# Summing the first batch's keys with products on both partition halves, a new order of the first tokens' attention, a third bank for expert 1, and two later pieces in other slots

## The chip, the cores and the metric

The kernel runs on one core of a Trainium2 chip. The metric is the device time of one execution in microseconds. A profile gives the span from the first to the last instruction, which is 1.5 to 2 us shorter than the timed figure; spans are compared with spans and times with times. A run counts as slow when it is over 1.5% above the fastest of the same kernel.

Engines are called PE (matrix products), DVE (VectorE), ACT (ScalarE) and POOL (GpSimd).

## The reference, cut to what matters

```python
# q, k, v: 8 batches, 8 heads, 576 tokens, 64 per head; four experts, 512 -> 1024 -> 512
k_p = k.reshape(B, H, Sp, 8, D).mean(axis=3)          # keys and values: means of 8 neighbours, 72 left
v_p = v.reshape(B, H, Sp, 8, D).mean(axis=3)
attn = softmax(q @ k_p^T / sqrt(D))
x = (attn @ v_p), heads side by side                  # 4608 tokens x 512
for e in range(4):
    out += p[:, e:e + 1] * (relu(x @ w1[e]) @ w2[e])  # "up" and "down" products
```

## The kernel before

The attention of the first 512 tokens (four rows of 128) runs before anything else. Nothing else is there for PE to do, because the first up products need its result. From then on the kernel walks chunks of tokens and experts. In each step PE does up and down products, and pieces of the next batch's attention are put into numbered slots between them. Most products are done by a scheme with seven block products in place of eight, for which DVE first adds or subtracts blocks of weights and of activations ("combine").

The first batch's keys lie on 64 partitions, nine neighbouring tokens in each. A 0/1 matrix (`takes`) sums groups of eight by nine accumulating products. The values already lie on both partition halves, and their products alternate between the halves:

```python
def sum_pool(raw, hs):                      # keys: one half of the partitions
    for h in range(hs.start, hs.stop, 2):
        s_ps = work_bank()
        for r in range(ROWS):               # ROWS = 9
            nc.tensor.matmul(s_ps[0:SP, 0:n], lhsT=takes[0:PR, r], rhs=raw[:, h:h + 2, r, :], ...)

def sum_values(g):                          # values: two halves, two banks, in turn
    banks = [work_bank()[0:SP, 0:n] for _ in range(2)]
    for r in range(ROWS):
        for half in range(2):
            ps = slice(half * PR, (half + 1) * PR)
            nc.tensor.matmul(banks[half], lhsT=takes[ps, r], rhs=raws[("vraw", 0)][ps, g, :, r, :], ...)

def idle(n):                                # dummy products; nothing reads their results
    w_ps = work_bank()
    for _ in range(n):
        nc.tensor.matmul(w_ps, lhsT=zeros[:, 0:P], rhs=zeros)
```

The order of the first attention, from the key sums on. `scores_first(group, tok)` does scores and exponential of four heads and 256 tokens; `context` and `context_half` do a row's products with the values and then a division on DVE; `turn` transposes a row for the up products:

```python
sum_keys(lo); keys(0, lo); sum_keys(hi); scores_first(0, 0); keys(0, hi)
sum_values(0); scores_first(1, 0); context_half(0, 0); sum_values(1)
scores_first(0, 1); turn_half(0, 0); context_half(0, 1); idle(3); turn_half(0, 1)
context(0, 1); scores_first(1, 1); up_first(range(0, 4), first)
turn(0, 1); context(0, 2); idle(1); up_first(range(0, 4), second); context(0, 3)
... # rest of up_first, turn(0, 2), turn(0, 3)
up(0, 0, range(FCH), half)                  # the second half: 256 tokens, 8 blocks
```

Two more places matter: the banks of the up products, and the slots of later pieces.

```python
banks = units[1] if n == NT else units[1] + chains[1:]      # 2 banks for 512 wide, 3 for 256 wide
...
turn_of("up", 2)                            # first_chunk: which of the two banks comes first
...
usual = dict(queries=-8, keys=-9, values=-2, ...)
plans[BUSY + 1] = dict(usual, values=4, v=(5, 8, 12, 16))   # fourth batch: its key fold in slot -9
... ((12, 15, 22, 19), weight_sums(2)) ...                  # the fourth combine of expert 2 in slot 19
```

The softmax here doesn't subtract the row's maximum and nothing guards it: scores larger than these inputs give would overflow.

## Time and profile before

| | before |
|---|---|
| time, median of the first 3 runs | 497.9 us (497.85 to 498.71) |
| span of the profile | 495.8 us |
| PE busy | 488.6 us, 99% |
| PE idle | 7.2 us |

The prediction below shows the lines on which it rests: the busy times, the chain, PE's timeline of the first 22 us and the one late wait. One view that it does not show is DVE's timeline where the first attention ends (start, length, engine and line, what, then the idle time before it and what ended it):

```profile
17.92 0.20 DVE L397 RECIPROCAL inv<-att_first 128x8 f32<-128x8 f32 x1
18.15 0.69 DVE L398 TENSOR_TENSOR x_tok<-att_first,inv 128x512 bf16<-128x512 f32 x1
19.47 0.21 DVE L397 RECIPROCAL inv<-att 128x8 f32<-128x8 f32 x1 [0.63 <-PE att L435]
19.71 0.69 DVE L398 TENSOR_TENSOR x_tok<-att,inv 128x512 bf16<-128x512 f32 x1
```

The reader sees the last two divisions (reciprocal and product, 0.9 us together). The third row's is over before the last row's can start: DVE waits 0.63 us for the last context.

### The profile page before, as it was taken

Reading aid. Unit: us, or ns where it says so; the run is one execution under the profiler, and the core shown is the slowest. Engines: PE = TensorE matmul, PEld = TensorE weight load, DVE = VectorE, ACT = ScalarE, POOL = GpSimd, SP = SyncE. Lnnn points to the kernel's source line nnn. Section 1 sums busy time; section 2 is a strip of 40 time slices with the busy share of each in tenths; the row PEclk is TensorE's granted clock in tenths of the full one; section 3 lists DMA queues with packets and bytes.
Section 4 is the critical chain, followed back from the end, with each engine's and each line's share of the span. In section 5 each row is a group of like instructions: output and inputs, shape, how many; then the busy total and the mean of one; then the engine's idle time right before and its main releaser. Section 6 shows DMA issues by size and latency. Waiting matters only on the chain.

```text
span 495.8 us, 11453 instructions
## 1 busy us (share of the span) xinstructions
PE 488.6 (99%) x4663; PEld 407.1 (82%) x4663; DVE 377.1 (76%) x756; ACT 302.7 (61%) x561; POOL 114.4 (23%) x112
## 2 busy tenths in 40 slices
PE   8999999999999999999999999999999999999996
PEld 5856468888888888888888888888888888888885
DVE  5567889799768975788669876896679766976674
ACT  4666536865685568656775667567665566556650
POOL 8230413232352154114421262111000100011010
PEclk9999999999999999999999999999999999999999
DMA  9999996998679659553974398130211010004003
GB/s 199 210 207 203 205 164 92 119 73 97 76 112 62 95 61 146 47 78 37 156 73 67 47 138 80 36 65 22 76 23 22 22 65 1 13 22 86 1 1 85
DMA packets 101779, 41.95 MB, mean 85 GB/s; under 512 B 73808, under 2 KB 100176, under 8 KB 101728
## 3 DMA queue, kind: packets, MB, share of 16 engines
q0 software_dynamic: 56896, 22.42, 40.4%
q1 hardware_dynamic: 43728, 17.77, 17.6%
q10 hardware_dynamic: 1104, 1.05, 0.6%
q8 instruction: 36, 0.59, 0.5%
q14 instruction: 15, 0.12, 0.1%
HBM read 45.69 MB, written 9.44 MB: 111 GB/s over the span
## 4 chain that ended last, share of the span: by engine, by line
PE 95%; DVE 2%; ACT 1%; issue 1%; ACTq 0%
PE o_ps L724 40%; PE unit L656 39%; PE unit L583 5%; PE o_ps L750 3%; PE att L382 2%; PE unit L332 1%; PE unit L782 1%; PE att L435 1%; DVE acc L799 1%; PE unit L598 0%; PE unit L306 0%; DVE H L637 0%; DVE kp L285 0%; PE att L489 0%; PE att L472 0%
## 5 line engine op out<-in xcount | busy, mean ns | idle before, releaser
L799 DVE SCALAR_TENSOR_TENSOR acc<-o_ps,p_all,acc 128x256 f32<-128x256 f32 (+1 forms) x285 | 127.1, 486 | 54.3 <-PE o_ps L724 36.1
L724 PEld LDWEIGHTS <-H 128*128 128x128 bf16 x1320 | 129.1, 98 | 16.2 <-issue 0.3
L656 PEld LDWEIGHTS <-w_bf 128*128 128x128 bf16 x1024 | 97.8, 98 | 15.9 <-issue 4.5
L637 DVE CUSTOM_DVE_ANT_0 H<-unit,partial 128x512 bf16<-128x512 f32 x128 | 87.4, 685 | 25.5 <-PE unit L656 20.9
L724 PE MATMUL o_ps<-w_bf,H 128*128 128x256 bf16 x792 | 102.6, 273 | 0.0
L656 PE MATMUL unit<-xT,w_bf 128*128 128x256 bf16 x672 | 96.4, 273 | 0.8 <-ACT unit L669 0.8
L671 ACT COPY partial<-unit 128x512 f32<-128x512 f32 x128 | 72.0, 589 | 33.2 <-PE unit L656 32.9
L738 POOL TENSOR_TENSOR acc<-acc,addend 128x512 f32<-128x512 f32 x24 | 30.4, 1265 | 258.3 <-ACT addend L736 201.3
L656 PEld LDWEIGHTS <-wu_bf 128*128 128x128 bf16 x768 | 73.3, 98 | 10.0 <-issue 1.5
L656 PE MATMUL unit<-xs,wu_bf 128*128 128x256 bf16 x512 | 76.9, 273 | 0.0
L724 PE MATMUL o_ps<-wt_bf,H 128*128 128x256 bf16 x528 | 68.4, 273 | 0.0
L724 PEld LDWEIGHTS <-S 128*128 128x128 bf16 x528 | 51.7, 98 | 6.4
L677 ACT ACTIVATE H<-unit 128x512 bf16<-128x512 f32 x64 | 38.2, 597 | 29.6 <-PE unit L656 29.3
L673 ACT ACTIVATE H<-unit 128x512 bf16<-128x512 f32 x64 | 38.8, 607 | 27.0 <-PE unit L656 27.0
L669 ACT COPY unit<-unit 128x512 f32<-128x512 f32 x64 | 37.4, 584 | 17.2 <-PE unit L656 14.7
L656 PE MATMUL unit<-xs,w_bf 128*128 128x256 bf16 x256 | 38.5, 273 | 0.0
L797 ACT ACTIVATE acc<-o_ps,p_all 128x256 f32<-128x256 f32 x72 | 30.2, 471 | 12.1 <-PE o_ps L724 10.8
L151 POOL DMA_DIRECT2D vraw<-in_v_dram x20 | 29.3, 1466 | 24.1 <-DMA vraw<-in_v_dram 23.8
L151 POOL DMA_DIRECT2D kraw<-in_k_dram x20 | 25.9, 1295 | 37.4 <-DMA kraw<-in_k_dram 37.4
L724 PE MATMUL o_ps<-wt_bf,S 128*128 128x256 bf16 x264 | 34.2, 273 | 0.0
L724 PE MATMUL o_ps<-w_bf,S 128*128 128x256 bf16 x264 | 34.2, 273 | 0.0
L656 PE MATMUL unit<-xT,wu_bf 128*128 128x256 bf16 x224 | 33.6, 272 | 0.0
(148 smaller groups left out, 516.7 us busy)
## 6 DMA issues: line engine op xcount, KB each, us to landing
out_dram<-acc SPq DMA_DIRECT2D x32, 256.0 KB, 4.2
w_bf<-in_moe_w_dram POOLq DMA_DIRECT2D x7, 1024.0 KB, 23.5
q_sb<-in_q_dram POOLq DMA_DIRECT2D x7, 512.0 KB, 9.8
vraw<-in_v_dram POOLq DMA_DIRECT2D x22, 144.0 KB, 6.5
kraw<-in_k_dram POOLq DMA_DIRECT2D x21, 144.0 KB, 5.3
w_bf<-in_moe_w_dram POOLq DMA_DIRECT2D x2, 512.0 KB, 8.8
wt_bf<-in_k_dram POOLq DMA_DIRECT2D x2, 288.0 KB, 6.8
wt_bf<-in_v_dram POOLq DMA_DIRECT2D x4, 144.0 KB, 5.6
```

The lines of the kernel that those rows point to most:

```text
L151: nc.gpsimd.dma_start(out=raw[:], in_=rows_of(src, b, 2 * part, 2 * part + 2), accum_op=ALU.add if part else ALU.bypass)
L583: nc.tensor.matmul(out_ps, lhsT=w1_bf[:, e, kc, fc * P:(fc + 1) * P], rhs=xT[:, kc, at], start=(kc == 0), stop=(kc == KC - 1), skip_group_ ...
L637: nc.vector._custom_dve(TENSOR_ADD_SAT, out=dst, in0=ps, in1=part, s0=LARGEST, s1=0.0)
L656: nc.tensor.matmul(ps[:, n * HN:(n + 1) * HN], lhsT=lhs[:, kc, f:f + P], rhs=rhs[:, kc, :], start=(not grows and n == 0 and kc == 0), stop ...
L669: nc.scalar.copy(out=units[unit][1][:], in_=ps)
L671: nc.scalar.copy(out=part[:, step - 2], in_=ps)
L673: nc.scalar.activation(out=quarter(0, 0), in_=ps, func=ACT.Relu)
L677: nc.scalar.activation(out=quarter(0, 1), in_=ps, func=ACT.Relu)
L724: nc.tensor.matmul(ps[:, j], lhsT=lhs[:, i, j * P:(j + 1) * P], rhs=rhs[:, i, :], start=(not grows and i == 0 and j == 0), stop=(i == HF - 1),
L738: nc.gpsimd.tensor_add(out=dst, in0=dst, in1=addend[:])
L797: nc.scalar.activation(out=dst, in_=o_ps, func=ACT.Copy, scale=prob)
L799: nc.vector.scalar_tensor_tensor(out=dst, in0=o_ps, scalar=prob, in1=dst, op0=ALU.mult, op1=ALU.add,)
```

## The change

Its intent is to take PE work out of the first stage, to start the up products earlier, and to remove the late wait. Its core:

```diff
-    def sum_pool(raw, hs):                    # nine products per pair of heads, one partition half
+    def sum_pool(nm, g):                      # keys now as the values: two halves, two banks, in turn
...
+                nc.tensor.matmul(banks[half], lhsT=takes[ps, r], rhs=raws[(nm, 0)][ps, g, :, r, :], ...)
...
+        copies = (nc.vector.tensor_copy, nc.scalar.copy if g else nc.vector.tensor_copy)   # values
... # keys loaded in four pieces instead of two, now on both halves; DVE makes the two halves of `takes`
... # at two places; context_half takes a fresh pair of banks per half
         sum_keys(0)
+        idle(1)
         keys(0, lo)
...
         sum_values(1)
+        turn_half(0, 0)
+        idle(1, chains[0][:])
+        context_half(0, 1)
         scores_first(0, 1)
-        turn_half(0, 0)
-        context_half(0, 1)
-        idle(3)
+        idle(1, chains[1][:])
         turn_half(0, 1)
         context(0, 1)
-        scores_first(1, 1)
         up_first(range(0, 4), first)
         turn(0, 1)
-        context(0, 2)
+        scores_first(1, 1)
         idle(1)
         up_first(range(0, 4), second)
+        context(0, 2)
         context(0, 3)
...
-            banks = units[1] if n == NT else units[1] + chains[1:]
+            banks = units[1] if e > 1 else units[1] + chains[1:]
...
-        turn_of("up", 2)
... # first_chunk: down products of expert 0 later, between the up products of experts 2 and 3
-        plans[BUSY + 1] = dict(usual, values=4, v=(5, 8, 12, 16))
+        plans[BUSY + 1] = dict(usual, keys=-8, values=4, v=(5, 8, 12, 16))
...
-        ... ((12, 15, 22, 19), weight_sums(2)) ...
+        ... ((12, 15, 22, 14), weight_sums(2)) ...
```

More of the change, by code (lines that the diff above doesn't have):

```diff
@@ L107, in choose_rows, with rows_chosen @@
         )
-        for half in range(2):
-            combine(takes[half * PR:(half + 1) * PR], begun[:, :, 0:SP], ALU.subtract, begun[:, :, 1:])
+    def rows_chosen(half):
+        combine(takes[half * PR:(half + 1) * PR], begun[:, :, 0:SP], ALU.subtract, begun[:, :, 1:])
     raws = {}
@@ L117, in groups, with load_whole, load_first @@
         return [slice(i * H // n, (i + 1) * H // n) for i in range(n)]
-    def load_whole(b, src, nm, parts=None):
-        rows = POOL if b else ROWS
+    def load_whole(b, src, nm):
         room = wt_bf[:, 1:E].rearrange("p e s i d -> p (e s i d)")
-        at = {"kraw": 0, "vraw": 1}[nm] * H * rows * D
-        raw = room[0:S // rows, at:at + H * rows * D].rearrange("j (h r d) -> j h r d", h=H, r=rows)
-        for hs in parts or groups(b):
+        at = {"kraw": 0, "vraw": 1}[nm] * H * POOL * D
+        raw = room[0:SP, at:at + H * POOL * D].rearrange("j (h r d) -> j h r d", h=H, r=POOL)
+        nc.gpsimd.dma_start(out=raw, in_=src[b].rearrange("h (j r) d -> j h r d", r=POOL))
+        raws[(nm, b)] = raw
+    def load_first(src, nm, g):
+        n = H // 2 * ROWS * D
+        at = {"kraw": 0, "vraw": 1}[nm] * n
+        room = wt_bf[:, 1:E].rearrange("p e s i d -> p (e s i d)")[:, at:at + n]
+        raw = raws[(nm, 0)] = room.rearrange("p (g h r d) -> p g h r d", g=2, h=2, r=ROWS)
+        for half in range(2):
+            h = 4 * g + 2 * half
             nc.gpsimd.dma_start(
-                out=raw[:, hs].rearrange("j h r d -> j h (r d)"),
-                in_=src[b, hs].rearrange("h (j r) d -> j h (r d)", r=rows),
-            )
-        raws[(nm, b)] = raw
-    def load_values_first():
-        at = H * ROWS * D
-        room = wt_bf[:, 1:E].rearrange("p e s i d -> p (e s i d)")[:, at:at + H // 2 * ROWS * D]
-        raw = raws[("vraw", 0)] = room.rearrange("p (g h r d) -> p g h r d", g=2, h=2, r=ROWS)
-        for g in range(2):
-            for half in range(2):
-                h = 4 * g + 2 * half
-                nc.gpsimd.dma_start(
-                    out=raw[half * PR:(half + 1) * PR, g].rearrange("j h r d -> j h (r d)"),
-                    in_=v[0, h:h + 2].rearrange("h (j r) d -> j h (r d)", r=ROWS),
-                )
+                out=raw[half * PR:(half + 1) * PR, g].rearrange("j h r d -> j h (r d)"),
+                in_=src[0, h:h + 2].rearrange("h (j r) d -> j h (r d)", r=ROWS),
+            )
     def rows_of(src, b, lo, hi):
@@ L298, in keys @@
         nc.vector.tensor_copy(out=state[("kpT", b)][:, hs, 0:SP], in_=kpt_ps[:, hs])
-    def sum_pool(raw, hs):
-        n = 2 * D
-        for h in range(hs.start, hs.stop, 2):
-            s_ps = work_bank()
-            for r in range(ROWS):
-                nc.tensor.matmul(s_ps[0:SP, 0:n], lhsT=takes[0:PR, r], rhs=raw[:, h:h + 2, r, :],
-                                 start=(r == 0), stop=(r == ROWS - 1))
-            yield slice(h, h + 2), s_ps[0:SP, 0:n].rearrange("j (h d) -> j h d", d=D)
-    def sum_keys(hs):
-        copies = (nc.vector.tensor_copy, nc.scalar.copy)
-        for copy, (part, kp) in zip(copies, sum_pool(raws[("kraw", 0)], hs), strict=True):
-            copy(out=kp_all[0:SP, part], in_=kp.unsqueeze(2).to_broadcast([SP, 2, 2, D]))
-    def sum_values(g):
+    def sum_pool(nm, g):
         n = 2 * D
@@ L320, in sum_values @@
                 ps = slice(half * PR, (half + 1) * PR)
-                nc.tensor.matmul(banks[half], lhsT=takes[ps, r], rhs=raws[("vraw", 0)][ps, g, :, r, :],
+                nc.tensor.matmul(banks[half], lhsT=takes[ps, r], rhs=raws[(nm, 0)][ps, g, :, r, :],
                                  start=(r == 0), stop=(r == ROWS - 1), skip_group_check=True)
@@ L324, in sum_values, with sum_keys, idle @@
             h = 4 * g + 2 * half
-            nc.vector.tensor_copy(out=vps[0][:, h:h + 2, 0:D],
-                                  in_=banks[half].rearrange("j (h d) -> j h d", d=D))
-    def idle(n):
-        w_ps = work_bank()
+            yield slice(h, h + 2), banks[half].rearrange("j (h d) -> j h d", d=D)
+    def sum_keys(g):
+        copies = (nc.vector.tensor_copy, nc.scalar.copy)
+        for copy, (hs, kp) in zip(copies, sum_pool("kraw", g), strict=True):
+            copy(out=kp_all[0:SP, hs], in_=kp.unsqueeze(2).to_broadcast([SP, 2, 2, D]))
+    def sum_values(g):
+        copies = (nc.vector.tensor_copy, nc.scalar.copy if g else nc.vector.tensor_copy)
+        for copy, (hs, vp) in zip(copies, sum_pool("vraw", g), strict=True):
+            copy(out=vps[0][:, hs, 0:D], in_=vp)
+    def idle(n, w_ps=None):
+        if w_ps is None:
+            w_ps = work_bank()
         for _ in range(n):
@@ L406, in context_half @@
             state[("x", 0, r)] = npool.tile([P, 2, NPAIR, D], BF16, name="x_tok", bufs=4)
-            state[("c", r)] = two_banks(0)
-        c_ps = state[("c", r)]
+        c_ps = two_banks(0)
         for i in range(NPAIR):
@@ L411, in context_half @@
             nc.tensor.matmul(
-                c_ps[:, g, at:at + D + 1],
+                c_ps[:, 0, at:at + D + 1],
                 lhsT=state[("expT", 0)][:, g * NPAIR + i, r // 2, r % 2, :],
@@ L415, in context_half @@
             )
-        divide(c_ps[:, g:g + 1], state[("x", 0, r)][:, g:g + 1])
+        divide(c_ps[:, 0:1], state[("x", 0, r)][:, g:g + 1])
     def turn_half(r, g):
@@ L528, in attention_first @@
         idle(14)
+        rows_chosen(0)
         round_q(0)
         round_q(1)
+        rows_chosen(1)
         queries(0, 0)
@@ L536, in attention_first @@
         idle(1)
-        sum_keys(lo)
+        sum_keys(0)
+        idle(1)
         keys(0, lo)
-        sum_keys(hi)
+        sum_keys(1)
         scores_first(0, 0)
@@ L842, in first_chunk @@
             up(0, 2, (i,))
-            if i == 1:
+            if i < 3:
+                sums[1][i]()
+                sums[2][i]()
+            if i == 3:
                 open_bank(chains[1][:])
                 each(*weight_sums(0))
-            if i >= 2:
-                down(0, 0, i - 2)
-                if i in (3, 4):
-                    hidden_sums(0, 0, i - 1)
-                if 4 <= i < 7:
-                    sums[1][i - 4]()
-                    sums[2][i - 4]()
-                if i == 5:
-                    sums[1][3]()
-                if i == 6:
-                    fold_keys(1, every)
-        down(0, 0, 6)
-        up(0, 3, (0, 1, 2))
+            if i >= 4:
+                down(0, 0, i - 4)
+                if i in (5, 6):
+                    hidden_sums(0, 0, i - 3)
+        sums[1][3]()
+        fold_keys(1, every)
+        for i in range(3):
+            up(0, 3, (i,))
+            down(0, 0, 4 + i)
         queries(1, 0)
@@ L863, in first_chunk @@
         queries(1, 2)
+        up(0, 3, (4,))
         queries(1, 3)
-        up(0, 3, (4,))
         keys(1, every)
@@ L964 @@
         load_q(0, 1)
-        load_whole(0, k, "kraw", groups(0)[:1])
-        load_whole(0, k, "kraw", groups(0)[1:])
+        load_first(k, "kraw", 0)
+        load_first(k, "kraw", 1)
+        choose_rows()
         make_identity(nc, ident[:])
-        choose_rows()
-        load_values_first()
+        load_first(v, "vraw", 0)
+        load_first(v, "vraw", 1)
         load_w1(0)
@@ L996 @@
         sums = {}
-        for at, pieces in (((3,), weight_sums(3)[3:]), ((7,), first_weight_sums(2)[3:]), ((8,), weight_sums(1)[3:]), ((12, 15, 22, 19), weight_sums(2)),
+        for at, pieces in (((3,), weight_sums(3)[3:]), ((7,), first_weight_sums(2)[3:]), ((8,), weight_sums(1)[3:]), ((12, 15, 22, 14), weight_sums(2)),
                            ((15,), first_weight_sums(3)[3:])):
```

## The prediction

> **What bounds the kernel now.** I read the page first, then the list of who waited for whom on TensorE, then the timelines of the first 22 us and of the one stretch with a wait.
>
> ```profile
> PE 488.6 (99%) x4663; PEld 407.1 (82%) x4663; DVE 377.1 (76%) x756; ACT 302.7 (61%) x561; POOL 114.4 (23%) x112
> ```
> ```profile
> PE 95%; DVE 2%; ACT 1%; issue 1%; ACTq 0%
> ```
>
> TensorE (PE) is busy for 488.6 of 495.8 us and carries 95% of the chain that ended last. Only two things can shorten the run: PE work taken away where PE is the bound, or one of its few waits. 7.2 us idle is the ceiling for waits, and part of that is before the first matmul and after the last.
>
> The first stage, up to about 22 us, is the one that the change is named after. PE's timeline:
>
> ```profile
> 8.15 1.19 PE L306 MATMUL unit<-wt_bf,S 64*72 64x128 bf16 x18
> 9.35 0.24 PE L297 MATMUL o_ps<-ident,kp 72*128 72x72 bf16 x2
> 9.80 0.24 PE L297 MATMUL o_ps<-ident,kp 72*128 72x72 bf16 x2 [0.21 <-ACT kp L313]
> 9.97 1.08 PE L306 MATMUL unit<-wt_bf,S 64*72 64x128 bf16 x16
> ...
> 11.79 0.69 PE L321 MATMUL unit<-wt_bf,S 64*72 64x128 bf16 x18
> ...
> 15.92 0.40 PE L515 MATMUL att<-qT,kpT 64*128 64x128 bf16 x8
> ...
> 20.77 0.39 PE L453 MATMUL att_first<-ident,x_tok 128*128 128x128 bf16 x4
> 20.99 0.61 PE L598 MATMUL o_ps<-xT,w_bf 128*128 128x128 bf16 x8
> 21.68 1.05 PE L583 MATMUL unit<-xT,w_bf 128*128 128x256 bf16 x8
> ```
>
> The columns are start, length, engine and line, what it does, and the idle time before it. L306 sums keys on one partition half, L321 sums values on both halves in turn. Most of the real waits of this stage are filled with dummy matmuls (L332), so they don't show as idle.
>
> After 22 us PE waits noticeably once. Who waited for whom on PE, 100 to 120 us, then VectorE (DVE) there, and the key fold's own line:
>
> ```profile
> PE unit L656 <- ACT unit L669: 0.8, 1, 0.8
> ```
> ```profile
> 109.42 1.26 POOL L738 TENSOR_TENSOR acc<-acc,addend 128x512 f32<-128x512 f32 x1 [4.13 <-ACT addend L736]
> 109.56 1.74 DVE L285 TENSOR_TENSOR kp<-kraw 72x512 bf16<-72x512 bf16 x2
> ...
> 111.23 0.68 DVE L242 TENSOR_TENSOR w_bf<-w_bf 128x1024 bf16<-128x1024 bf16 x1
> 111.83 0.67 DVE L637 CUSTOM_DVE_ANT_0 H<-unit,partial 128x512 bf16<-128x512 f32 x1
> ...
> 112.59 0.57 ACT L669 COPY unit<-unit 128x512 f32<-128x512 f32 x1 [2.41 <-DVE H L637]
> 113.21 0.27 PE L656 MATMUL unit<-xT,w_bf 128*128 128x256 bf16 x1 [0.79 <-ACT unit L669]
> ```
> ```profile
> L285 DVE TENSOR_TENSOR kp<-kraw x12: 408/414/1409, 81.1 to 318.5; 72x512 bf16<-72x512 bf16 x12
> ```
>
> PE waits for a ScalarE (ACT) copy, which waits for L637 on DVE, which sits behind two key folds and a weight combine. The folds take 1.74 us there. Their median is 0.41 us and the slowest of 12 took 1.41; that slow one lies beside an addition on POOL.
>
> **What the Trainium skill says.** "TensorEngine Tiling (Array Packing)", section Tiling Modes: products on separate row tiles load and multiply in parallel; Restrictions and Gotchas: they must write different PSUM banks. The trace agrees: 18 products on one half hold PE from 8.15 to about 9.18 (57 ns apart), 18 that alternate halves and banks from 11.79 to 12.33, when the next scores start: 0.54 against 1.03 us.
> "SBUF — State Buffer", section Who interferes with whom: a DVE instruction with two SBUF inputs contends with a GpSimd instruction that reads SBUF, and the one that comes second blocks. The fold has two SBUF inputs, the POOL addition reads SBUF and started 0.14 us earlier: 1.41 us in place of 0.41 agrees.
> "DMA: Bandwidth & Descriptors", Queues, rings and completion order: each engine takes the descriptors of a ring in order. So splitting the key load in four should not move the bytes behind it. The trace is consistent: the page shows 199 to 210 GB/s in each of the first five slices, and from issue and landing the key halves are in at 7.7 and 9.2 us, the value pieces at 10.0 to 12.2, the first weights from 14.7 on.
>
> **The change, part by part.**
> *Key sums.* 2 x 18 products go from 1.03 to 0.54 us: 0.98 us less PE work. The dummy matmuls number 21 before and after.
> But the stage is a chain of hand-offs, so I walk it with durations of before. Sum 0 still starts at 8.15, behind the query transposes. Its copies start at 8.87 (0.73 after the sum's start, as for the values) and end at 9.29. The new dummy matmul reuses the bank that DVE is reading, so it waits until 9.35 and the transposes begin at 9.57 (the last two began at 9.80). Sum 1: 9.81 to 10.35. Scores 10.35 to 10.68; copies 10.54 to 10.96; transposes 11.02. Value sum 0: 11.27 (11.79 before). First context 12.34 (12.86). Value sum 1: 12.69 (13.21). So 0.5 us ahead at this point.
> Then the new order spends it. The first turn now comes straight after value sum 1 and waits for the division until 13.57; second context 13.90; second turn, after its division, 15.02 (15.44); context of row 1 at 15.14; first up products about 15.5 to 16.5. Turn of row 1 waits for its division to 16.65, and only then come the last scores, at 16.87 (15.92 before). Their exponential (1.02 us) ends at 18.44; contexts of rows 2 and 3 from 18.5; two divisions of 0.9 us each on DVE to 20.7; turn of row 3 at 20.76 (20.77 before); its copy to 21.6; the second half of the up products at about 21.65 (21.68).
> So the early gain is largely lost to the later scores: 0.1 us left, as my estimate, with 0.4 either way because six hand-offs are each known to 0.1 at best.
> *Third bank for expert 1.* At 25.1 PE lost 0.2 us when it went over to expert 1 with two banks, the wanted one being still read by ACT. A third bank takes that away: 0.2 us.
> *Down products later, between the third and fourth experts' up products.* As much PE work as before. PE shows no wait there now, and the arrival of the second layer's first weights at 33.6 is left further behind. 0.
> *Keys of the fourth batch one slot later, one weight combine from slot 19 to 14.* DVE before the L637 at 111.83 loses 1.67 us of folds and 0.60 of combine, so that L637 runs at about 109.56. ACT's copy then follows PE's own product (110.96), ends at 111.6, and PE goes on at 112.26 instead of 113.21: 0.95. The folds now come behind the two accumulations, at about 111.35. POOL's addition ended at 110.68, so they should take 0.67 instead of 1.67. The next L637 then ends at 113.3, the accumulations at 114.1, the copy of the output bank at 114.8, about when PE wants it (114.88). A further 0.15 us before the down products at 115.98 goes too, less 0.1 for closeness. Sum: 1.0. In slot 14 the combine fits: DVE waited 0.77 us at 102.0.
> *Sum.* 0.1 + 0.2 + 0 + 1.0 = 1.3 us; 497.9 - 1.3 = 496.6 us.
>
> **The rivals.**
> *All of the product saving reaches the end.* The 0.98 us less work would then give 497.9 - (1.0 + 0.2 + 1.0) = 495.7. For it: the order was surely tuned for this. Against: the scores 0.95 us later, with exponential, contexts and two divisions behind them in series.
> *The stall moves instead of going.* If the folds are slow at the new place too (1.67 us), the next L637 ends at 114.3 and the output bank's copy at 115.7: PE wins only 0.2 of the 1.1 us there, and the time is 497.4. For it: DVE is busy without a break from 102.7 to 119. Against: no POOL addition lies at 111.35.
> *Transfers take over.* Keys come in four pieces, values are issued some 0.6 us later. If the stream slips by that, the values' second half (landing about 12.2, wanted at 12.7) and the first weights would hold PE, and the stage would be 0.3 to 0.5 us slower than now: 497.0 to 497.2 with the other gains. Against: the queue works through bytes without a pause, and the issues stay ahead of it. The later weights have slack: expert 1's are in at 23.7 and wanted at 25; the second layer's of expert 1 are in at 53.6 and wanted at 54.9 in the kernel before. The latter also caps what could be carried past that point at about 1.4 us.
>
> **Range and chances.** The best case is 495.7; a stall that moves and a stage that gains nothing give 497.6. The three runs of before spread over 0.86 us, mostly upwards. I take 495.7 to 497.6. 2% would be 10 us, more than all idle time of PE, and no rival adds a tenth of that: faster 0.005, same 0.99, slower 0.005.
>
> **What would show the steps right or wrong.** PE's timeline: key sums of about 0.55 us each; value sum 0 near 11.3; the last scores near 16.9; the second half of the up products within 0.4 of 21.65; no gap near 25. In the list of waits: no PE wait for L669 (then another line number) near 112, and key folds of 0.41 us each at the new place. DMA: landings of weights as before. The prediction fails if the folds meet POOL again, if the up products' second half starts before 21.2, or if a wait on a weight load appears.

## The result, and the profile after

| | before | after |
|---|---|---|
| time, median of 6 runs each | 497.88 us (497.3 to 498.71) | 496.25 us (495.8 to 497.87) |
| ratio after/before | | 0.9969, 95% interval 0.9951 to 0.9987: "same" at 2% |
| span of the profile | 495.8 us | 494.2 us |

A ratio here is the mean time of one kernel's fast runs over that of the other's of the same rounds (in the experiments without the first run of each), so it is not quite the ratio of the medians quoted. The changed kernel is 0.3% faster, and the interval excludes 1.

The page after, busy times and then the chain:

```profile
PE 486.7 (98%) x4656; PEld 405.9 (82%) x4663; DVE 375.9 (76%) x755; ACT 302.9 (61%) x562; POOL 115.8 (23%) x114
```
```profile
PE 98%; DVE 1%; issue 0%; DVEq 0%
```

PE's share of the chain went from 95 to 98%, and DVE's from 2 to 1%: a detour of the chain is gone. In the kernel before the chain ran over ACT and DVE from 100 to 113.2 us; now it stays on PE there. PE is busy 1.9 us less by the page, but seven of its product records are missing there (4656 against 4663), so this figure is not exact. PE's timeline of the first stage after:

```profile
7.92 0.69 PE L302 MATMUL unit<-wt_bf,S 64*72 64x128 bf16 x18
9.12 0.38 PE L323 MATMUL unit<-H 128*128 128x512 bf16 x1 [0.51 <-DVE kp L311]
...
11.07 0.69 PE L302 MATMUL unit<-wt_bf,S 64*72 64x128 bf16 x18
...
16.70 0.40 PE L505 MATMUL att_first<-qT,kpT 64*128 64x128 bf16 x8
...
17.29 1.05 PE L592 MATMUL unit<-xT,w_bf 128*128 128x128 bf16 x16
18.18 0.42 PE L425 MATMUL att<-vp,expT 72*128 72x65 bf16 x8
...
21.39 1.05 PE L577 MATMUL unit<-xT,w_bf 128*128 128x256 bf16 x8
```

The key sum is as short as the value sum (both 0.69 us with the modelled end of the last product). The value sum starts 3.15 us after the first key sum instead of 3.64. Yet the last line, the second half of the up products, starts 13.46 us after the key sum instead of 13.53. Half a microsecond is gained at the start of the stage and gone again at its end.

DVE around the late stall, and the key fold's own line, after:

```profile
109.07 0.68 DVE L631 CUSTOM_DVE_ANT_0 H<-unit,partial 128x512 bf16<-128x512 f32 x1
...
110.76 0.75 DVE L281 TENSOR_TENSOR kp<-kraw 72x512 bf16<-72x512 bf16 x2
```
```profile
L281 DVE TENSOR_TENSOR kp<-kraw x12: 409/415/420, 80.6 to 316.9; 72x512 bf16<-72x512 bf16 x12
```

The operation that PE's next product needs (L631) now starts at 109.07, before the folds, and the folds take 0.75 us together. The slowest of the 12 folds is 0.420 us; it was 1.409. PE's list of waits between 20 and 130 us is empty.

**Aligning the traces.** The first query transposes start at 6.51 us before and at 6.29 after, although nothing ahead of them changed on PE. Among all profiles they start anywhere from 6.06 to 7.14. The reason is in the first line of PE's timeline, the 14 dummy products at the start; here in the kernel before and in that of the second experiment:

```profile
1.26 5.42 PE L332 MATMUL unit<-H 128*128 128x512 bf16 x14 [1.26 <-DVE H L818]
```
```profile
1.26 6.04 PE L332 MATMUL unit<-H 128*128 128x512 bf16 x14 [1.26 <-DVE H L818]
```

The same 14 products take 5.42 and 6.04 us here (5.20 in the changed kernel), because more or fewer of them run 427 ns apart before they go to 216 ns. The Trainium skill says this in "TensorE: Matmul & The Clock Gate", Part 1: The HAM clock gate: 426.7 ns cold and 215.7 ns warm at this width, and a window that runs freely, so that the change-over varies from run to run. The traces agree in both spacings. In the eleventh experiment, the earliest, the change-over comes with the seventh product, which starts at 3.79 us; in the second, the latest, with the fourteenth, which starts at 6.78 us. So it moved by some 3.0 us: more than the 0.5 us either way that the page gives for it, but in line with its counts of 6, 11 or 14 cold products in runs of one kernel. (The query transposes of the eleventh then waited for DVE, so their own spread, 1.08 us, is less than seven products would give.) So every stage below is measured from a mark inside the same trace, not from its start:

| us | before | after | gain |
|---|---|---|---|
| start to first key sum | 8.15 | 7.92 | 0.22 (chance, above) |
| first key sum to second half of up products | 13.53 | 13.46 | 0.07 |
| from there to expert 1's first up product | 3.70 | 3.50 | 0.20 |
| from there to the loop of chunks | 48.10 | 48.09 | 0.01 |
| the loop, to the remainder chunk | 360.46 | 359.37 | 1.09 |
| first key sum to end | 487.62 | 486.25 | 1.38 |

The lengths are rounded from finer times, so a sum can be off by 0.01. The loop is counted from its first product with combined activations (`unit<-xs,wu_bf`), 3.9 us after its very first one.

### The profile page after: what moved, and what is told of

It is laid out like the page before. It is cut to its first block, busy times and chain, and to the rows that moved or that the text cites. A ratio compares the mean times of both kernels' runs of the same rounds, so it can differ in the third digit from the quotient of the medians.

```text
span 494.2 us, 11449 instructions
## 1 busy us (share of the span) xinstructions
PE 486.7 (98%) x4656; PEld 405.9 (82%) x4663; DVE 375.9 (76%) x755; ACT 302.9 (61%) x562; POOL 115.8 (23%) x114
## 4 chain that ended last, share of the span: by engine, by line
PE 98%; DVE 1%; issue 0%; DVEq 0%
PE o_ps L718 41%; PE unit L650 40%; PE unit L577 4%; PE o_ps L744 3%; PE att L373 2%; PE att L425 2%; PE unit L323 1%; PE unit L776 1%; PE o_ps L577 1%; PE unit L592 0%; PE unit L302 0%; PE att L479 0%; PE att L462 0%; PE att_first L443 0%; PE o_ps L592 0%
## 5 line engine op out<-in xcount | busy, mean ns | idle before, releaser
L631 DVE CUSTOM_DVE_ANT_0 H<-unit,partial 128x512 bf16<-128x512 f32 x128 | 87.5, 686 | 25.5 <-PE unit L650 20.9
```

Source lines behind the costliest of these rows:

```text
L631: nc.vector._custom_dve(TENSOR_ADD_SAT, out=dst, in0=ps, in1=part, s0=LARGEST, s1=0.0)
```

## The experiments

All twelve kernels gave correct results. Those with three rounds have four runs of their own beside seven of the kernel before; the others ran once. The stage lengths, from the profiles:

| kernel | time, us | key sum to second half | second half to expert 1 | loop | key sum to end |
|---|---|---|---|---|---|
| before | 497.88 | 13.53 | 3.70 | 360.46 | 487.62 |
| after | 496.25 | 13.46 | 3.50 | 359.37 | 486.25 |
| e1_late_only | 496.63 (4 runs) | 13.53 | 3.70 | 359.64 | 486.81 |
| e2_keys_only | 498.09 (1) | 13.53 | 3.70 | 360.45 | 487.60 |
| e3_combine_only | 497.34 (1) | 13.52 | 3.70 | 360.46 | 487.62 |
| e4_no_pool_there | 498.58 (1) | 13.52 | 3.70 | 361.50 | 488.66 |
| e5_two_banks | 497.23 (1) | 13.47 | 4.14 | 359.37 | 486.92 |
| e6_scores_early | 496.07 (1) | 13.75 | 3.50 | 359.36 | 486.57 |
| e7_no_reused_bank | 496.51 (1) | 13.20 | 3.50 | 359.48 | 486.39 |
| e8_old_order | 495.65 (4) | 12.71 | 3.50 | 359.38 | 485.53 |
| e9_tail_old | 496.74 (1) | 13.28 | 3.50 | 359.73 | 486.43 |
| e10_head_old | 497.07 (1) | 13.13 | 3.50 | 360.27 | 486.85 |
| e11_two_banks_turn | 496.42 (1) | 13.47 | 3.70 | 359.79 | 486.90 |
| e12_queries_behind | 495.50 (4) | 13.19 | 3.51 | 359.36 | 486.52 |

The last kernel does part of its query work behind the first key sum, so its lengths from the key sum are not to be compared with the others'; it is measured from the first query transposes instead, further below.

**A second stall, which comes and goes.** Some loops are longer for a reason that no edit touches. At 94 us PE waits for the exponential of the scores in seven of the fourteen profiles. By the gap between its products these are 0.37 (e1), 0.70 (e3), 1.13 (e4), 0.20 (e7), 0.46 (e9), 1.01 (e10) and 0.53 us (e11), of which about 0.1 us is the gap in an undisturbed profile. The others, with before and after among them, don't show it. Here is the list of waits of the fourth experiment, 80 to 100 us (total, times, longest), and then the stores that ACT waited for, as a row of the sum's tile (issues on the store queue; ns least, median and longest; first and last start), in the kernel before and in the fourth experiment:

```profile
ACT acc L797 <- DMA out_dram<-acc: 1.7, 1, 1.7
...
PE att L382 <- ACT expT L386: 1.0, 1, 1.0
```
```profile
L807 SPq DMA_DIRECT2D out_dram<-acc x3: 373/431/532, 83.2 to 85.8; - x3
```
```profile
L807 SPq DMA_DIRECT2D out_dram<-acc x3: 372/532/1747, 83.3 to 85.9; - x3
```

One of three stores of the running sum took 1.75 us to issue instead of at most 0.53, and landed at about 92 us instead of 88.7 us. ACT may not overwrite that part of the sum before. The fifth and the eighth show the slow issue too (1.602 us each), with waits of 0.6 and 0.7 us on ACT that PE does not feel. Why the issue is slow in some executions stays open. It is there in kernels with each edit and missing in others with the same edits, so I treat it as chance; one profile of each cannot prove that. Below, the loop is judged by its waits near 112 us and not only by its length.

Runs are called e1 to e12 below, by the table.

### The late part

**Both edits of the late part alone, on the kernel before.**

```diff
-        plans[BUSY + 1] = dict(usual, values=4, ...)
+        plans[BUSY + 1] = dict(usual, keys=-8, values=4, ...)
-        ... ((12, 15, 22, 19), weight_sums(2)) ...
+        ... ((12, 15, 22, 14), weight_sums(2)) ...
```

> The kernel before with only the two later moves: the fourth batch's key folds one slot later, and the weight combine from slot 19 to slot 14. Theory (the stall near 112 us is the larger half of the gain and does not depend on the first stage): no PE wait near 112, both key folds 0.41 us each, the span 1.0 to 1.15 us below the run of before once both are aligned at the start of the key sums. Rival (the stall goes only because PE arrives at another time after the changed first stage): the wait of about 0.9 us stays, and the span is within 0.2 us of before.

Measured: 496.63 us against 497.96 us before (ratio 0.997, interval 0.9954 to 0.9987). No PE wait near 112 us; the slowest fold took 0.421 us. The loop is 0.82 us shorter, and would be about 1.09 us shorter without the store's wait (0.37 us, some 0.27 above the normal gap). (As it was measured, the span is 0.81 us below that of before from the key sum on; 1.0 to 1.15 had been expected.) So the late part alone gives most of the change's gain.

**Only the key fold one slot later.**

```diff
-        plans[BUSY + 1] = dict(usual, values=4, ...)
+        plans[BUSY + 1] = dict(usual, keys=-8, values=4, ...)
```

> The kernel before with the key folds of the fourth batch one slot later, the combine left at slot 19. Theory (the folds are 1.67 of the 2.27 us that stood ahead of the DVE instruction PE waits for, so they alone do it): that DVE instruction starts near 110.2, no PE wait of over 0.1 us, aligned gain 0.9 to 1.1 us. Rival (both moves are needed): PE still waits 0.3 us or more, gain about 0.6.

Measured: a loop of 360.45 us, so no gain at all. My expectation missed. DVE's timeline there, then POOL's, then PE's waits:

```profile
110.16 1.68 DVE L242 TENSOR_TENSOR w_bf<-w_bf 128x1024 bf16<-128x1024 bf16 x1
111.76 0.68 DVE L637 CUSTOM_DVE_ANT_0 H<-unit,partial 128x512 bf16<-128x512 f32 x1
...
113.15 0.74 DVE L285 TENSOR_TENSOR kp<-kraw 72x512 bf16<-72x512 bf16 x2
```
```profile
110.03 1.26 POOL L738 TENSOR_TENSOR acc<-acc,addend 128x512 f32<-128x512 f32 x1 [4.72 <-ACT addend L736]
```
```profile
PE unit L656 <- ACT unit L669: 0.3, 1, 0.3
PE o_ps L724 <- ACT o_ps L732: 0.2, 1, 0.2
```

The combine, which had stood behind the folds, now stands where they stood. It too has two inputs in SBUF, starts 0.13 us after POOL's addition, and takes 1.68 us instead of 0.68. The block of 1.0 us passes from one operation to the next in line, and PE's wait comes back in parts: as gaps between its products, 0.28, 0.47 and 0.35 us, together the 1.10 us that it waited before (0.95 and 0.15).

**Only the combine moved to slot 14.**

```diff
-        ... ((12, 15, 22, 19), weight_sums(2)) ...
+        ... ((12, 15, 22, 14), weight_sums(2)) ...
```

> The kernel before with the combine moved to slot 14, the key folds left. Theory: DVE sheds 0.6 us ahead of the instruction that PE waits for, the first fold still takes 1.41 us beside the POOL addition, PE waits about 0.35 us in place of 0.95; aligned gain 0.5 to 0.65. Rival (the fold then escapes POOL by timing): fold 0.41 us and the gain about 1.0.

Measured: the wait near 112 us falls from 0.95 to 0.35 us as the gap between PE's products, so 0.60 us, one combine, is gained there as expected. The span doesn't show it, because the store's wait at 94 us took 0.6 us more. The fold is as slow as before:

```profile
L285 DVE TENSOR_TENSOR kp<-kraw x12: 411/413/1408, 81.0 to 318.3; 72x512 bf16<-72x512 bf16 x12
```

**The POOL addition taken away at that place,** by letting DVE accumulate that block too, as it does most others.

```diff
-                down(*below_of[t2], i2, t2 % 2, POOLED)
+                down(*below_of[t2], i2, t2 % 2, () if t2 == 2 else POOLED)
```

> The kernel before, but the one accumulation that runs on POOL beside the folds (1.26 us at 109.4) is done by two DVE instructions in its place. Theory (the POOL addition and the fold contend): both folds take 0.41 us; DVE pays 0.8 us for the two accumulations and gets 1.0 back, so PE's wait near 112 shrinks by only about 0.2. Rival (the fold is slow for another reason, such as its input just landed or the transposing transfers beside it): one fold still takes about 1.4 us, and PE's wait grows by 0.8 us.

Measured: nothing else in DVE's order there changes, and the fold is back at its normal length:

```profile
L285 DVE TENSOR_TENSOR kp<-kraw x12: 411/412/423, 81.2 to 319.5; 72x512 bf16<-72x512 bf16 x12
```

This shows that the POOL addition made the fold slow. The fold also starts 1.8 us later here, but a fold that comes too soon after its input landed is no rival: in e3 it starts 2.8 us after the keys' last landing (107.25 us) and takes 1.408 us, in the changed kernel also 2.8 us after it (107.98 us) and takes 0.414 us; transposing transfers run beside both. PE's wait near 113 us is 0.27 us shorter than before (0.2 was expected), with the two accumulations more on DVE. The span is 1.0 us worse all the same: the store's wait at 94 us was at its longest here (1.03 us above the normal gap), and PE has a gap of 0.28 us at 207.7 us that no other profile has and whose cause is open.

### Expert 1's banks

**Two banks for expert 1 again,** on the changed kernel; first without, then with the spare step of the turn count that the kernel before had.

```diff
-            banks = units[1] if e > 1 else units[1] + chains[1:]
+            banks = units[1] if n == NT else units[1] + chains[1:]
```

> The changed kernel with expert 1's up products of the first batch back on two banks. Theory (the third bank took away a wait of 0.2 us at the change-over from expert 0 to expert 1): a gap of about 0.2 us on PE near 25 us again, and the rest unchanged, so 0.2 us longer between the first wide up product and the loop. Rival (the gap went for another reason): no gap, same length.

Measured: 4.14 us from the second half to expert 1, 0.64 more than after, though 0.2 was expected. PE's wait:

```profile
PE unit L577 <- ACT H L582: 0.5, 1, 0.5
```

The edit had left out that the change also removes `turn_of("up", 2)`. With two banks, it decides which of them comes first: here the one that had been filled last, which ACT was still to read. So the run mixed two things, and the next one puts the step back.

```diff
             banks = ... as above ...
+        turn_of("up", 2)
         sums = {e: first_weight_sums(e) for e in range(E)}
```

> The changed kernel with two banks for expert 1 and with the spare count of the bank turn put back, which the change had also removed, so that the first bank is the one that the kernel before took. Theory (the earlier two-bank run paid 0.63 us because it began with the bank that ScalarE reads last; the wait of 0.2 us belongs to two banks as such): a wait of 0.2 us on PE near 25 us, 3.70 us from the first 256-wide to the first 512-wide up product against 3.50 changed and 4.14 in the two-bank run. Rival: 4.1 again.

Measured: 3.70 us, exactly as before. The third bank is worth 0.20 us, and with two banks the right one first is worth 0.44 us (4.14 less 3.70).

### The first stage

**The last scores back ahead of the first up products.**

```diff
         context(0, 1)
+        scores_first(1, 1)
         up_first(range(0, 4), first)
         turn(0, 1)
-        scores_first(1, 1)
         idle(1)
```

> The changed kernel with the last scores of the first batch moved back before the first up products, as in the kernel before. Theory (the late scores put their exponential, two contexts and two divisions in series at the end of the stage and cost what the paired products had won): the exponential ends near 17.0 in place of 18.2, the wait before the third row's turn goes, and the time from the start of the key sums to the first 256-wide up product falls from 13.47 to 13.0 to 13.2 us. Rival (other hand-offs or the arrival of the weights are the bound): it stays within 0.1 us of 13.47.

Measured: 13.75 us, 0.29 us worse than after. The expectation missed. The scores are 1.27 us earlier counted from the key sum (7.51 us after it instead of 8.78), but the contexts of the last two rows stand behind the second group of up products in PE's order, and this group starts 9.65 us after the key sum instead of 9.36: the scores, 0.33 us of PE, now stand ahead of row 1's turn, which it needs. In the changed kernel the late exponential (17.14 to 18.16 us) ends just as that group does (contexts at 18.18 us). So two bounds end together there, and taking the late scores away alone gains nothing.

**The dummy product taken out of the bank that DVE is reading.**

```diff
         sum_keys(0)
-        idle(1)
         keys(0, lo)
```

> The changed kernel without the one dummy product after the first key sum, which waits for a bank that DVE is still reading. Theory: the key transposes begin about 0.25 us earlier after the sum, and as the chain of hand-offs behind it is tight at first, most of it, 0.1 to 0.25 us, is still there at the first 256-wide up product (13.47 before it). Rival (waits for the values' arrival or for the weights take it up): the transposes are earlier, but the first 256-wide up product is not.

Measured: 13.20 us, 0.26 us gained, as expected. In the end 0.28 us of it was spent at 47 us, where PE waited for an accumulation on DVE. The changed first chunk puts the fold of the second batch's keys ahead of that accumulation, and the keys landed at 43.66 us against 42.16 in the profile after.

**The whole old order with the new sums.**

```diff
         sum_keys(0)
-        idle(1)
         keys(0, lo)
...
         sum_values(1)
+        scores_first(0, 1)
         turn_half(0, 0)
-        idle(1, chains[0][:])
         context_half(0, 1)
-        scores_first(0, 1)
-        idle(1, chains[1][:])
+        idle(3)
         turn_half(0, 1)
         context(0, 1)
+        scores_first(1, 1)
         up_first(range(0, 4), first)
         turn(0, 1)
-        scores_first(1, 1)
+        context(0, 2)
         idle(1)
         up_first(range(0, 4), second)
-        context(0, 2)
         context(0, 3)
```

> The changed kernel with the paired key sums kept, but contexts, turns, scores and dummies of the first stage in the order of the kernel before. Theory (the new order, not the paired sums, is why 0.98 us less PE work gave 0.06 us): from the start of the key sums to the first 256-wide up product 12.6 to 13.0 us in place of 13.47 (changed) and 13.53 (before), and the timed median 0.4 to 0.9 us below the changed kernel. Rival (the stage is bound by hand-offs or landings in either order): 13.3 to 13.5 us and no difference in time. The arrival of the second weights of expert 1 (53.6 us) may take part of it back.

Measured: 12.71 us, 0.75 less than after and 0.82 less than before. Time 495.65 us against 497.87 before (ratio 0.9954, interval 0.9937 to 0.9972). So the paired sums do carry most of their 0.98 us to the end of the stage, but only in the old order. (This run keeps the changed key load and value copies too, and no run has the paired sums alone. But 0.76 of the 0.82 us is there already when the first value sum starts, 2.88 us after the key sum instead of 3.64.) PE with the old order:

```profile
8.53 0.69 PE L302 MATMUL unit<-wt_bf,S 64*72 64x128 bf16 x18
...
16.94 0.42 PE L425 MATMUL att<-vp,expT 72*128 72x65 bf16 x8
...
17.62 1.05 PE L590 MATMUL unit<-xT,w_bf 128*128 128x128 bf16 x16
...
21.24 0.94 PE L575 MATMUL unit<-xT,w_bf 128*128 128x256 bf16 x7
```

The context of row 2 (16.94) now comes before the second group of up products (17.62). DVE at the end of the stage, first in the changed kernel, then with the old order:

```profile
18.64 0.21 DVE L388 RECIPROCAL inv<-att 128x8 f32<-128x8 f32 x1 [1.40 <-PE att L425]
...
19.49 0.20 DVE L388 RECIPROCAL inv<-att_first 128x8 f32<-128x8 f32 x1
```
```profile
17.48 0.20 DVE L388 RECIPROCAL inv<-att 128x8 f32<-128x8 f32 x1
...
19.04 0.21 DVE L388 RECIPROCAL inv<-att_first 128x8 f32<-128x8 f32 x1 [0.63 <-PE att_first L425]
```

In the changed kernel DVE sits idle for 1.40 us until 18.64, which is 10.72 us after the first key sum, and then does both divisions in a row. In the old order the first of them starts 8.95 us after the key sum (17.48 less 8.53), and only one is left at the end. The last division starts 10.51 us after the key sum instead of 11.57.

**Only the tail of the order old** (from `context(0, 1)` on), and **only the head old** (up to it):

```diff
# tail old, on the changed kernel           # head old, on the changed kernel
+        scores_first(1, 1)                 -        idle(1)             (after sum_keys(0))
         up_first(range(0, 4), first)       +        scores_first(0, 1)  (after sum_values(1))
         turn(0, 1)                                  turn_half(0, 0)
-        scores_first(1, 1)                 -        idle(1, chains[0][:])
+        context(0, 2)                               context_half(0, 1)
         idle(1)                            -        scores_first(0, 1)
         up_first(range(0, 4), second)      -        idle(1, chains[1][:])
-        context(0, 2)                      +        idle(3)
         context(0, 3)                               turn_half(0, 1)
```

> The changed kernel with only the second half of the first stage in the old order: last scores before the first up products, and the context of row 2 before the second quarter of them. Theory (moving the scores alone did not help, because both contexts stayed behind the second quarter and their divisions stand in series there; both must move): DVE does the division of row 2 about 1.2 us earlier, and the time from the start of the key sums to the first 256-wide up product falls from 13.46 to about 13.1. Rival (only the first half of the stage matters): 13.4 to 13.75, as with the scores alone.

> The changed kernel with only the first half of the first stage in the old order (scores of the first group before the first turn, no dummy on a bank in use, dummies three in a row), and the second half as changed. Theory: the second turn is 0.3 to 0.4 us earlier; about 13.1 us from the start of the key sums to the first 256-wide up product. With the tail's 0.35 the two add up to the 0.75 of the whole old order. Rival (the serial divisions at the end set the time whatever comes before): 13.4.

Measured: 13.28 us (0.19 gained, half of what was expected) and 13.13 us (0.33 gained, as expected), together 0.52 of the 0.75 us. Neither half explains the loss alone, and the two are not additive. The rest, 0.23 us, appears only when both are old. One more mark, the first product of the second group of up products, takes the lengths apart:

| us | before | after | e6 | e7 | e8 | e9 | e10 |
|---|---|---|---|---|---|---|---|
| key sum to second group | 9.91 | 9.36 | 9.65 | 9.10 | 9.09 | 9.65 | 9.03 |
| from there to second half | 3.62 | 4.10 | 4.10 | 4.10 | 3.62 | 3.62 | 4.10 |

The second length has two values: 3.62 us where the context of row 2 stands before the group, 4.10 us where both contexts stand behind it. So the tail costs 0.48 us, and the new head 0.28 us (9.36 less 9.09). With the old tail and the new head (e9), 0.29 us of the 0.48 is lost again because the last scores stand ahead of row 1's turn, as in e6. With the old head they cost only 0.06 us (9.09 less 9.03): they start earlier (6.96 us after the key sum instead of 7.52), and the turn waits for its division until 8.06 us anyway. The cause of these two figures is read from the timelines; no run isolates it. Both loops have the store's wait at 94 us, so their times say nothing against this.

**The old order, and two of the four query pairs behind the first key sum.**

```diff
         queries(0, 1)
-        idle(2)
-        queries(0, 2)
-        queries(0, 3)
         idle(1)
         sum_keys(0)
+        queries(0, 2)
+        queries(0, 3)
         keys(0, lo)
```

> The kernel with paired sums and the old order, and in addition the transposes of the third and fourth pair of queries moved behind the first key sum, where PE waits 0.5 us for the copies, with three dummy products fewer ahead of it. Theory (the stage is a chain of hand-offs that starts with the key sum, and the keys are in at about 7.5 us): from the first query transposes to the first 256-wide up product 13.6 to 13.9 us in place of 14.34, and a timed median 0.2 to 0.6 us below that of the old order. Rival (the arrival of values and first weights is the bound by now): the same length within 0.2 us, with PE waiting on a landing.

Measured: from the first query transposes to the second half 14.04 us, against 14.34 (21.24 less 6.90) with the old order alone. So 0.30 us is gained in this stage, less than expected. Two dummy products fewer than in the old order stand ahead of the key sum (0.43 us of PE), so the gain can't be put to the moved queries alone. It is not more because the first key sum now starts before its data are all there (the second piece landed at 7.60 us):

```profile
PE unit L302 <- DMA wt_bf<-in_k_dram: 0.3, 1, 0.3
```

About 0.5 us is lost again near 46 us, where the second batch's keys and the accumulations are waited for. Time 495.50 us against 498.35 before (ratio 0.995, interval 0.9932 to 0.9968). This kernel and that of the old order both beat the two kernels by their medians (496.25 and 497.88). Against the kernel before, both intervals exclude 1. Against the changed one, the intervals overlap, and the difference rests on the aligned first stage. Between the two of them the times decide nothing.

## Why the prediction was right

The prediction was 496.6 us and the median 496.25, within its range of 495.7 to 497.6, and in the class "same". By its own sum:

| term | predicted gain | measured |
|---|---|---|
| first stage | 0.1 | 0.07 |
| third bank for expert 1 | 0.2 | 0.20, confirmed by e11 |
| down products later | 0 | 0.01 |
| late part | 1.0 | 1.09, confirmed by e1 but for the store's wait |
| sum | 1.3 | 1.38 from the key sum to the end |

The remaining 0.22 us of the difference between the two profiles is the start. The medians differ by 1.63 us, close to the profiles' 1.60 us, though the start's share in the unprofiled runs isn't known. That the median came within 0.35 us of the forecast is partly luck: single runs of one kernel spread over 1.4 us (before) and 2.1 us (after). And by the prediction's own terms its upper end would be 497.5 (0.2 for the bank, 0.2 for the stall), not 497.6.

**The walk through the first stage** can be held against the trace step by step, both counted from the first key sum (us):

| step | predicted | measured |
|---|---|---|
| dummy product may start | 1.20 | 1.20 |
| value sum 0 | 3.12 | 3.15 |
| value sum 1 | 4.54 | 4.57 |
| second turn, first row | 6.87 | 6.88 |
| context of the second row | 6.99 | 7.00 |
| last scores | 8.72 | 8.78 |
| turn of the last row | 12.61 | 12.55 |
| second half of the up products | 13.50 | 13.46 |

Every step of the table was right to 0.06 us, with durations from the kernel before and hand-offs in place of busy times.

**What the walk said of the cause was only partly right.** It put the loss down to the later last scores, with exponential, contexts and divisions in series behind them. The serial divisions are there. But e6 moved those scores back and lost 0.29 us more. What the new order costs is 0.48 us for the third row's context behind the second group of up products (e8, e9) and 0.28 us for the head, of which its dummy product on a bank in use is 0.26 (e7). Where I wrote "the order was surely tuned for this" in favour of the first rival, e8 shows the opposite: the new order costs 0.75 us of the 0.82 that the stage gains with the paired sums and the old one. The rival's full 0.98 us was nearly there to be had, by not reordering.

**The late part** was right in mechanism and nearly in size. The fold is slow because of POOL's addition (e4), the PE wait goes (e1), and the folds are normal at their new place. The times agree too: L631 at 109.07 us and the folds at 110.76 us are 109.56 and 111.25 us counted as in the kernel before (its loop starts 0.49 us later), where 109.56 and 111.35 were predicted. The rival that the stall moves did not come about in the changed kernel, but it was closer than its wording let one think: with the fold moved and the combine left, it did (e2). The gain depends on both edits.

**The transfers** did not take over. The first weights landed at 14.65 us against 14.73 before, the second layer's first weights at 33.65 against 33.59. Here the Trainium skill's ordering of a ring (cited in the prediction) agrees: the pieces landed in the order of issue, keys at 6.93, 7.58, 8.06 and 8.72 us, values from 9.46 to 11.66. What I had not foreseen is that the two groups of keys were usable earlier: at 7.58 and 8.72 us instead of 7.73 and 9.22. All nine profiles with the changed load show it (7.26 to 7.60 and 8.61 to 8.94 us, against 7.65 to 8.13 and 9.16 to 9.45 in the other five). The change both split the load and put it on other partitions, and no run separates the two.

## What to carry to other kernels

When work is taken out of a stage that is a chain of hand-offs, change the work and the order separately and measure each, because a new order can spend what the work saved. When an operation is blocked by a neighbour on a shared port, moving that one operation may only hand the block to the next of its kind; look at what will stand in its place. Align traces at a mark inside the kernel before tenths of a microsecond are compared, and look for waits that come and go between executions.

## What the Trainium skill lacked or had wrong

- "SBUF — State Buffer", Who interferes with whom: agrees that a two-input DVE operation behind a POOL operation that reads SBUF is blocked. The page has no duration for such a pair: here the block was 1.0 us for a fold (1.409 against 0.414 us) and 1.0 us for a combine (1.68 against 0.68), each started 0.13 to 0.14 us into a POOL addition of 1.26 us.
- "TensorEngine Tiling (Array Packing)", Tiling Modes: says that row tiles work in parallel; the page gives a theoretical factor of up to 2, but no measured duration for accumulating pairs. Here 18 products of 128 columns, alternating halves and banks, held PE for 0.54 us against 1.03 us on one half, 1.9 times less.
- "DMA: Bandwidth & Descriptors" has nothing that I could find on a store whose issue takes far longer in some executions: 1.60 to 1.95 us against at most 0.53 (one store of three near 84 us), landing some 3 us later, and up to 1.0 us of PE wait.
- "TensorE: Matmul & The Clock Gate", Part 1: The HAM clock gate: gives 0.5 us either way for the change-over of the clock, though its counts of 6, 11 or 14 cold products allow for more. Here it moved by some 3.0 us between profiles of kernels with the same first products (starts of 3.79 and 6.78 us, seven and fourteen slow products), and the first query transposes with it by up to 1.08 us.
